# Expert and feed-forward work ordered with shorter matmul durations and no charge for a change of TensorE's array shape

## The chip, the cores and the metric

One core of one Trainium2 chip. The metric is the device time of one execution, in microseconds (us). The time before is 448.63 us, the median of 3 runs (446.47 to 449.24). TensorE appears in the trace as PE (matmuls) and PEld (weight loads), VectorE as DVE, ScalarE as ACT, GpSimd as POOL, and SyncE, which issues most of the transfers, as SP.

## The reference

Three layers, each feeding the next, on 1152 tokens of width 512:

```python
local = softmax(causal(q @ k.T / 8)) @ v                  # 2 x 8 heads, 576 tokens, width 64
out   = g * (phi(q) @ M_prev) / (phi(q) @ z_prev) + (1 - g) * local
e     = argmax(x @ w_gate)                                # one of 8 experts for each token, capacity 288
x     = gate_w * (relu(x @ w1[e]) @ w2[e])                # w1[e] 512 x 1024, w2[e] 1024 x 512
out   = ((x @ w_a) * (x @ w_b)) @ w_out                   # w_a, w_b 512 x 1536, w_out 1536 x 512 
```

The last layer's matrices are held as 64-bit numbers and arrive as pairs of 32-bit words.

## The kernel before

Attention and gating take the first 190 us or so and stay as they are. Then the experts run in an order that is set by how many tokens each has (a rank from 0 to 7; rank 0 is computed beside the attention), and then the feed-forward layer on the tokens that were kept. The program holds several versions of this part, for different token counts; the one that runs here is for up to 816 tokens with the last rank empty.

Of the experts that this part computes, rank 1 is "big" and split (each matmul operand is a high and a low part, and a product is three matmuls, lines 903 to 905, 288 columns wide); rank 2 is big in plain float32 (lines 1398 and 1434); ranks 3 to 6 are "few" (line 1491): the few tokens are the stationary operand in a slice of the array, 64 columns of it for rank 3 and 32 for ranks 4 to 6, and the result is turned by transposes (line 1500) after ACT has copied it out of PSUM (line 1496). Rank by rank, `few` has the steps fx (tokens turned, line 1479), f1 twice (first layer, one per half of w1), bt (transposes), fh (relu, line 1524), f2 twice (second layer), fy (copy out), bt, st and sl (high and low part into x2, lines 915 and 918).

The feed-forward layer goes over three blocks of 512 hidden columns (i = 0, 1, 2) and two stripes of tokens, 512 and 304 wide. For each block the halves of w_a, w_b and w_out (1 MB each) are loaded, rebuilt as float32 by ACT and DVE (s0 on ACT, line 1301; s1 to s3 on DVE, lines 1305 to 1315; then a high part on ACT, line 915, and a low part on DVE, line 918). For each stripe come four products pa with w_a and four pb with w_b, 12 matmuls each, then c1 (ACT copies pa out, line 1605), c2 (DVE multiplies with pb, line 1608), c3 and c4 (high and low part), and the products with w_out (om, or po in the last block; lines 1629 to 1631), added up by lines 1637 and 1639.

All of this is entered as a list of operations into a planner, `Plan`. Each operation has an engine, a duration, a key (a due time), the operations that it follows, and the buffers that it takes and uses. `Plan.run` picks operations one after the other by the engines' planned clocks and by key, and the instructions are emitted in that order. Each engine runs its instructions in order, so an instruction that waits holds up all that stand behind it on that engine. `Plan` also decides which of the load buffers (raw0, raw1, raws0, raws1, rawd0, rawd1 and three more) a transfer gets, and so which earlier operation must have ended before the transfer can be issued. Operations of `few` carry the mode 64 or 32, the others 0; where an operation's mode is not that of the one before on its engine, `run` adds `self.change` to the planned start.

Of the kernel before, what the change touches and what calls it, by code (L numbers as in the profile page):

```python
# [29 lines left out]
            w=280.2, w_=-166)  # L30
GK = 0.0
AHEAD_ = 0.094
CHANGE = 0.25
# [16 lines left out]
AH2 = 0.7  # L50
# [100 lines left out]
def fused_kernel(  # L151
# [350 lines left out]
    def stacked(i):  # L502
        return STACK and i == NF_
# [348 lines left out]
    def token_ids(key):  # L852
        nc.vector.tensor_tensor(out=big, in0=oh, in1=rs[:, 6][:, None, :].to_broadcast([128, NTT, E]), op=ALU.mult)
        nc.vector.reduce_sum(out=dst, in_=big, axis=AX.X)
        nc.vector.tensor_tensor(out=dst, in0=dst, in1=pos, op=ALU.add)
        nc.vector.tensor_tensor(out=dsi, in0=dst, in1=over, op=ALU.add)
        for t in range(NTT):
            M = rows[t % NT]
            scatter("id" + key, id_d, dsi[:M, t:t + 1], tid[:M, t:t + 1], N)
# [106 lines left out]
    for n, (b, p) in enumerate(pairs):  # L966
# [35 lines left out]
        for i in UNITS:  # L1002
            u = n, i
            at_ = n * UP + UNITS.index(i)
            W, one = 128 * i + rows[i], stacked(i)
# [41 lines left out]
    for b in range(B):  # L1047
        last = b == B - 1
        n = (b + 1) * NP - 1
        G = GROUPS if last else [(0, NT)]  # L1050
        for i in range(NT):
            t = b * NT + i
# [178 lines left out]
    class Way:  # L1231


        def __init__(self, pool, x2, more, buffers, held=()):

            self.x2, self.pool = x2, pool
            self.buffers = dict(buffers, raw=raw_cells, bank=banks,
                                u=[pool.tile([128, 2, 512], I32, name=f"u{n}") for n in range(2)])
            self.buffers["part"] = parts_ + self.buffers.get("part", [])
            self.held, self.tile = dict(held), {}  # L1240
            self.plan = Plan(dict({k: len(t) for k, t in self.buffers.items()}, any=more), AH2, ("raw", "part"), CHANGE)
            for b, slot in self.held.items():
                self.plan.hold(b, slot)
            self.op, self.stored = {}, []
# [111 lines left out]
        def big(self, r, c0, w, exact, key, f, kinds):  # L1356
# [1 line left out]

            job = r, c0
            cost = max(0.214, 1.667e-3 * w) if exact else 3.0e-3 * max(256, w) / 7.2 + 0.002  # L1360
            cost = cost if exact else 3 * (max(256, w) / 2400.0 + 0.0125)
            self.tokens(r, job, w, c0, key - 10, "raw")
            xs, xt, ht = ("xs", job), ("xt", job), ("ht", job)
            got = []
# [20 lines left out]
            t = key + f * 0.11 * 4 * -(-w // 128)  # L1385
# [173 lines left out]
        def forward(self, W, key, t, before):  # L1559
# [8 lines left out]
            tiles = cut(-(-W // 128))  # L1568
            for i in range(NI3):
                s_ = slice(512 * i, 512 * i + 512)  # L1570
                A, Bq, O = ((c, i) for c in "abo")
                A, Bq, O = (("ff", c, i) for c in "abo")
                per = sum(12 * (max(256, min(128 * n, W - 128 * sum(tiles[:g]))) / 2400.0 + 0.013) for g, n in enumerate(tiles))
                lasts = [0.0, 0.0]
                blocks_ = {}
                c0 = 0

                w0 = min(128 * tiles[0], W)
                one = 12 * (w0 / 2400.0 + 0.013)
                need = {A: t, Bq: t + (4 * one if i == 0 else one), O: t + 8 * one}  # L1580
                for blk, src in ((A, w_a[:, s_]), (Bq, w_b[:, s_]), (O, w_out[s_, :])):
                    blocks_[blk] = self.wide(blk, src, need[blk], None)
                for gi, n in enumerate(tiles):
                    w = min(128 * n, W - c0)
                    c = 12 * (max(256, w) / 2400.0 + 0.013)
                    early_ = i == 0 and gi == 0

                    def half(b, blk, m, w=w, c0=c0):
# [6 lines left out]
                    for m in range(4):  # L1595
                        a, b, av, g = (k_ + (i, gi, m) for k_ in (("pa",), ("pb",), ("av",), ("g",)))
# [68 lines left out]
    def cut(T):  # L1665
        n = -(-T // 4)
        return [T // n + (1 if j < T % n else 0) for j in range(n)]
# [58 lines left out]
    def general(exact):  # L1726
# [11 lines left out]
        with room("x2p") as xp:  # L1738
            x2 = xp.tile([128, KD, 2, N + max(256, -(-top // 32) * 32)], F32R, name="x2")
            for kk in range(KD):  # L1740
                nc.gpsimd.memset(x2[:, kk].bitcast(F32), 0.0)
            with room("mp") as mp, room("wp") as wp:
                h_ = mp.tile([128, 4, 2, SW], F32R, name="h_")
                buffers = {"xte": [mp.tile([128, KD, 128], F32, name="xte")],
                           "he": [[t[:, m] for m in range(8)] for t in [mp.tile([128, 8, 128], F32, name="he")]],
                           "xt": [xt0], "h": [[h_[:, m] for m in range(4)] + [h1[:, m] for m in range(4)]]}
                way = Way(wp, x2, 1, buffers)
                way.limited, t = False, 0.0
                for p in range(E):
                    small = exact and LIMITS[p] >= 5  # L1750
                    for c0 in [0] if small else range(0, top, SW):
                        way.big(RANKS[p], c0, 128 if small else min(SW, top - c0), small, t, 1.0,
                                ["xte" if small else "xt", "he" if small else "h"])
                        t += 30.0
                way.plan.run()
            choose(kept, [768, 960, N], forward)
# [41 lines left out]
```

## Time and profile before

| | us |
|---|---|
| median of 3 runs | 448.63 |
| the profiled execution | 454.4 |
| its span, first to last instruction | 452.6 |
| PE busy in the span | 407.4 |
| DVE busy in the span | 266.8 |
| ACT busy in the span | 208.4 |

The trace is of one execution, which took 454.4 us, 5.8 more than the median; 1.8 us of it lie outside the span. Start times in the rows count from the start of the span. A matmul's busy time overlaps the next one's, so what a stream of matmuls takes is read from the distance of their starts.

### The profile page before, as it was taken

The page shows a single profiled execution, that of the slowest core. Times are in us where ns is not written, and L with a number is a line of the kernel's source. Part 1 is how long each engine was busy: PE and PEld are TensorE (multiplying, and loading weights), DVE is VectorE, ACT ScalarE, POOL GpSimd, SP SyncE. Part 2 cuts the span into 40 slices and gives each one's busy share as a digit, 9 for nine tenths or more (in the row PEclk, how much of TensorE's full clock was granted, in tenths as well). Part 3 has the DMA queues.
Part 4 walks back from the last instruction along what each step waited for, and adds up shares of the span by engine and source line. Part 5 has one row for each costly group of instructions (what it writes and reads, how often), then busy time and mean ns, then how long its engine had stood idle before and what let it go on. Part 6 is the DMA issues. An engine that isn't in the chain of part 4 may idle for free.

```text
span 452.6 us, 7884 instructions
## 1 busy us (share of the span) xinstructions
PE 407.4 (90%) x2868; PEld 355.4 (79%) x2868; DVE 266.8 (59%) x639; ACT 208.4 (46%) x451; POOL 104.7 (23%) x182
## 2 busy tenths in 40 slices
PE   6789998988799999497799986999999999999993
PEld 6667887967687999485598964888978889788892
DVE  4567775598774685354035017686297883967231
ACT  3767887478875541352044033453355504434010
POOL 8683676056700004127000000000000000000202
PEclk9999998999989979699889996999999999999997
DMA  3688999837961005399999999924034000000101
GB/s 76 135 178 126 244 287 302 196 87 253 257 245 37 1 2 218 116 390 209 160 363 387 386 393 407 405 98 150 37 101 170 10 0 1 1 1 0 71 25 59
DMA packets 59912, 74.48 MB, mean 165 GB/s; under 512 B 33955, under 2 KB 33955, under 8 KB 59856
## 3 DMA queue, kind: packets, MB, share of 16 engines
q1 hardware_dynamic: 58016, 70.48, 51.0%
q0 software_dynamic: 1632, 3.31, 2.1%
q8 instruction: 27, 0.44, 0.4%
q14 instruction: 29, 0.24, 0.2%
q10 hardware_dynamic: 208, 0.01, 0.0%
HBM read 58.75 MB, written 11.64 MB: 156 GB/s over the span
## 4 chain that ended last, share of the span: by engine, by line
PE 42%; DMA 9%; issue 4%; POOL 1%; ACT 1%; POOLq 0%; SPq 0%
PE bank L903 9%; PE bank L904 9%; PE bank L905 9%; DMA rawd<-in_moe_w_dram 5%; PE bank L1629 3%; PE bank L1630 3%; PE bank L1631 3%; DMA raw<-in_moe_w_b_dram 3%; PE bank L1434 2%; PE bank L1491 2%; DMA raw<-xs_d 2%; POOL out_dram L762 1%; PE bank L1500 0%; PE bank L1479 0%; PE bank L912 0%
## 5 line engine op out<-in xcount | busy, mean ns | idle before, releaser
L905 PE MATMUL bank<-x,part 128*128 128x512 f32 (+1 forms) x192 | 67.6, 352 | 0.0
L903 PE MATMUL bank<-x,part 128*128 128x512 f32 (+1 forms) x160 | 56.7, 354 | 0.4 <-ACT x L915 0.4
L904 PE MATMUL bank<-x,part 128*128 128x512 f32 (+1 forms) x160 | 56.5, 353 | 0.0
L762 POOL DMA_INDIRECT out_dram<-c,ids x4 | 3.9, 986 | 200.3 <-DVE c L1639 196.8
L569 ACT ACTIVATE a<-sv,mn 128x128 f32<-128x128 f32 (+4 forms) x72 | 41.9, 584 | 16.5 <-DVE mn L549 15.5
L549 DVE CUSTOM_DVE_ANT_0 sv<-psS,mask 128x128 f32<-128x128 f32 (+4 forms) x72 | 34.5, 516 | 9.9 <-PE psS L533 7.6
L905 PEld LDWEIGHTS bank<-x,part 128*128 128x128 f32 x192 | 36.7, 191 | 4.3
L903 PEld LDWEIGHTS bank<-x,part 128*128 128x128 f32 x160 | 30.7, 192 | 4.5 <-issue 0.7
L904 PEld LDWEIGHTS bank<-x,part 128*128 128x128 f32 x160 | 30.8, 192 | 4.0 <-DVE x L918 0.2
L584 PE MATMUL psB<-ident,a 128*128 128x128 f32 x200 | 31.0, 282 | 2.3 <-ACT a L569 1.8
L1608 DVE TENSOR_TENSOR c<-c,bank 128x512 f32<-128x512 f32 (+1 forms) x24 | 13.9, 579 | 31.3 <-PE bank L905 30.9
L601 ACT COPY at<-psB 128x512 f32<-128x512 f32 (+2 forms) x48 | 23.7, 511 | 11.5 <-PE psB L584 9.0
L584 PEld LDWEIGHTS psB<-ident,a 128*128 128x128 f32 x200 | 23.8, 144 | 6.2 <-ACT a L569 3.4
L1605 ACT COPY c<-bank 128x512 f32<-128x512 f32 (+1 forms) x24 | 12.0, 500 | 27.5 <-PE bank L905 21.8
L915 ACT CAST a<-c 128x512 fp32r<-128x512 f32 (+1 forms) x12 | 6.4, 534 | 35.6 <-DVE c L1608 30.0
L611 PE MATMUL psC<-at,ldv 128*64 128x256 f32 (+1 forms) x192 | 19.9, 349 | 0.6 <-ACT at L601 0.6
L762 POOL DMA_INDIRECT xs_d<-x,di x10 | 10.5, 1046 | 40.8 <-DVE ggt L723 34.0
L533 PE MATMUL psS<-d 128*128 128x256 f32 (+2 forms) x56 | 16.1, 363 | 3.9 <-DMA d<-s 2.5
L918 DVE TENSOR_TENSOR part<-u,part 128x1024 fp32r<-128x1024 f32 x14 | 17.1, 1220 | 3.4 <-issue 1.9
L1305 DVE TENSOR_SCALAR u<-u 128x1024 f32<-128x1024 f32 x18 | 12.4, 687 | 11.2 <-ACT u L1301 11.2
L611 PEld LDWEIGHTS psC<-at,ldv 128*64 128x64 f32 x192 | 12.7, 136 | 7.2 <-issue 1.3
L918 DVE TENSOR_TENSOR x<-bank,x 128x160 f32 (+3 forms) x12 | 3.9, 363 | 22.7 <-ACT x L915 22.7
(293 smaller groups left out, 1105.3 us busy)
## 6 DMA issues: line engine op xcount, KB each, us to landing
raw<-in_moe_w_dram SPq DMA_DIRECT2D x16, 1024.0 KB, 9.9
rawd<-in_moe_w_dram SPq DMA_DIRECT2D x6, 1024.0 KB, 13.6
raws<-in_moe_w_dram SPq DMA_DIRECT2D x6, 1024.0 KB, 13.2
xs_d<-h SPq DMA_DIRECT2D x10, 512.0 KB, 3.9
d<-s SPq DMA_DIRECT2D x14, 288.0 KB, 3.5
rawd<-in_moe_w_a_dram SPq DMA_DIRECT2D x3, 1024.0 KB, 7.6
raw<-in_moe_w_b_dram SPq DMA_DIRECT2D x3, 1024.0 KB, 19.9
raws<-in_moe_w_out_dram SPq DMA_DIRECT2D x3, 1024.0 KB, 10.4
```

Source lines behind the costliest of these rows:

```text
L533: nc.tensor.matmul(sc[:M, h, 0:w], lhsT=l_, rhs=r_, start=j == 0, stop=j == 2)
L549: nc.vector.tensor_tensor_reduce(out=o, in0=i0, in1=i1, scale=1.0, scalar=3.0e38, op0=ALU.add, op1=ALU.min, accum_out=mn[:M])
L569: nc.scalar.activation(out=st[u, "a"][:M, h, 0:W], in_=sv[:M, 0:W], func=AF.Exp, scale=-1.0, bias=mn[:M], **more)
L584: nc.tensor.transpose(pt[:kr, M * j:M * j + M], a_t[:M, h, 128 * kt:128 * kt + kr], ident[:M, :M])
L601: eng(out=st[n, a, "at"][:, h0:h0 + nh, 0:i + 1, c0:c0 + 128], in_=pt[:, 0:m * 128].rearrange("p (h k m) -> p h k m", h=nh, m=128))
L611: nc.tensor.matmul(po[64 * h:64 * h + 64, c0:256], lhsT=vt[:, kt, h, 0:D], rhs=at_[:, h, kt, c0:256], start=kt == 0, stop=kt == 2 * a + 1)
L762: ins = nc.gpsimd.indirect_dma_start(out=out_[:, :], out_offset=bass.IndirectOffsetOnAxis(ap=idx, axis=0), in_=in_, in_offset=None, bounds ...
L903: nc.tensor.matmul(out_, lhsT=wh, rhs=xh, start=first, stop=False)
L904: nc.tensor.matmul(out_, lhsT=wh, rhs=xl, start=False, stop=False)
L905: nc.tensor.matmul(out_, lhsT=wl, rhs=xh, start=False, stop=last)
L918: (eng or nc.vector).tensor_tensor(out=to, in0=src, in1=hi, op=ALU.subtract)
L1608: nc.vector.tensor_tensor(out=self[av][:, 0:w], in0=self[av][:, 0:w], in1=self[b][:, 0:w], op=ALU.mult)
```

## The change

The planner for the experts and the feed-forward layer is made without the charge for a change of mode (0.25 us before, 0 now; the attention's planner keeps it), and three durations are shorter by 0.0098 or 0.010 us for each matmul. For a 512-wide feed-forward product that is 12 x (512/2400 + 0.003) in place of 12 x (512/2400 + 0.013) planned us; the due times (keys) of the feed-forward layer are sums of these and so shrink too. No instruction is added or removed in what runs; engines, shapes and data are the same.

```diff
-            self.plan = Plan(dict({k: len(t) for k, t in self.buffers.items()}, any=more), AH2, ("raw", "part"), CHANGE)
+            self.plan = Plan(dict({k: len(t) for k, t in self.buffers.items()}, any=more), AH2, ("raw", "part"))
...
-            cost = cost if exact else 3 * (max(256, w) / 2400.0 + 0.0125)
+            cost = cost if exact else 3 * (max(256, w) / 2400.0 + 0.0027)
...
-                one = 12 * (w0 / 2400.0 + 0.013)
+                one = 12 * (w0 / 2400.0 + 0.003)
...
-                    c = 12 * (max(256, w) / 2400.0 + 0.013)
+                    c = 12 * (max(256, w) / 2400.0 + 0.003)
```

Up to the start of the part for experts and feed-forward the instructions of every engine stand as before. In that part the first visible place is on ACT, where the experts end and the feed-forward layer begins. Before, in a row, from the last store of the rank-1 expert: line 1496 is fy, line 1524 fh, line 1301 s0 of w_b, lines 881 and 915 with x2 the store of the last expert, line 1605 c1:

```order
L915 COPY x2_4548<-bank4_2605 128x288
L1496 COPY c_4552<-bank2_2603 128x128
L1301 ACTIVATE u0_4554<-raws0_1917 128x1024
L1524 ACTIVATE c_4552<-bank3_2604 128x128
L1301 ACTIVATE u1_4555<-raw0_208 128x1024
L1496 COPY c_4552<-bank7_2608 128x128
L881 TENSOR_LOAD nums_204
L915 ISA
L915 COPY x2_4548<-bank5_2606 128x4x32
L915 CAST xt0_214<-u0_4554 128x1024
L1605 COPY c_4552<-bank0_2601 128x512
```

The same place of ACT after the change:

```order
L915 COPY x2_4549<-bank4_2605 128x288
L1496 COPY c_4553<-bank5_2606 128x128
L881 TENSOR_LOAD nums_204
L915 ISA
L915 COPY x2_4549<-bank1_2602 128x4x32
L1301 ACTIVATE u0_4555<-raw0_208 128x1024
L1605 COPY c_4553<-bank2_2603 128x512
L1301 ACTIVATE u1_4556<-raw2_5375 128x1024
L1605 COPY c_4553<-bank7_2608 128x512
L915 CAST part3_213<-u0_4555 128x1024
```

The two s0 of w_b now stand behind the last expert's copy and store; its relus (line 1524) have all moved up ahead of this piece, and the second s0 stands behind the first c1.

The second place is PE at the same point: the products of the experts of rank 5 and 6 (line 1491, 16 matmuls a row) and their transposes (line 1500), up to the first pa. Before:

```order
L1491 MATMUL bank2_2603<-raws1_2585,c_4552 32x128 x16
L1491 MATMUL bank2_2603<-rawd1_2593,c_4552 32x128 x16
L1491 MATMUL bank3_2604<-raw1_209,c_4552 32x128 x16
L1500 MATMUL bank5_2606<-ident_126,c_4552 128x128
L1500 MATMUL bank7_2608<-ident_126,c_4552 128x128
L1491 MATMUL bank2_2603<-rawd0_1977,c_4552 32x128 x16
L1500 MATMUL bank3_2604<-ident_126,c_4552 128x128
L1491 MATMUL bank7_2608<-raw1_5193,c_4552 32x128 x16
L1491 MATMUL bank7_2608<-raw0_5224,c_4552 32x128 x16
L1500 MATMUL bank5_2606<-ident_126,c_4552 128x128
L903 MATMUL bank0_2601<-x2_4548,part1_211 128x512
```

After, from one product further up:

```order
L1491 MATMUL bank2_2603<-raw1_209,c_4553 32x128 x16
L1500 MATMUL bank1_2602<-ident_126,c_4553 128x128
L1491 MATMUL bank7_2608<-raws1_2585,c_4553 32x128 x16
L1491 MATMUL bank5_2606<-rawd0_1977,c_4553 32x128 x16
L1491 MATMUL bank5_2606<-rawd1_2593,c_4553 32x128 x16
L1500 MATMUL bank1_2602<-ident_126,c_4553 128x128
L1500 MATMUL bank2_2603<-ident_126,c_4553 128x128
L1500 MATMUL bank7_2608<-ident_126,c_4553 128x128
L1491 MATMUL bank5_2606<-raw0_5238,c_4553 32x128 x16
L1491 MATMUL bank5_2606<-raw1_5281,c_4553 32x128 x16
L1500 MATMUL bank1_2602<-ident_126,c_4553 128x128
L903 MATMUL bank2_2603<-x2_4549,part1_211 128x512
```

Both f1 of rank 6 now come ahead of both f2 of rank 5; the last pair of products, the last transpose and the first pa follow each other as before.

The third place is ACT in the first block of the feed-forward layer; it shows in which order PE delivers (line 1605 copies pa out, line 1637 adds up the products with w_out). Before:

```order
L1605 COPY c_4552<-bank6_2607 128x512
L915 CAST h1_97<-c_4552 128x512
L915 CAST part3_213<-u1_4555 128x1024
L915 CAST h1_97<-c_4552 128x512
L1605 COPY c_4552<-bank0_2601 128x304
L1301 ACTIVATE u1_4555<-raw1_209 128x1024
L1637 COPY c_4552<-bank1_2602 128x512
```

After:

```order
L1605 COPY c_4553<-bank0_2601 128x512
L915 CAST h1_97<-c_4553 128x512
L1605 COPY c_4553<-bank3_2604 128x304
L915 CAST h1_97<-c_4553 128x512
L1605 COPY c_4553<-bank4_2605 128x304
L915 CAST part0_210<-u1_4556 128x1024
L1301 ACTIVATE u1_4556<-rawd0_1977 128x1024
L915 CAST a_4551<-c_4553 128x304
L915 CAST part2_5659<-u0_4555 128x1024
L1605 COPY c_4553<-bank1_2602 128x304
```

On PE two of the 304-wide pa of the second stripe stand right behind the four 512-wide pa, ahead of the first pb, and all but one product of the second stripe ahead of the first stripe's products with w_out; before, the first pb came after four pa, and the products with w_out after nine products in all. In blocks i = 1 and 2 PE's order is unchanged.

Earlier, among the experts: PE computes three of the rank-1 expert's last four products (b2, 24 matmuls each) ahead of the second layer of rank 4, where before it computed one there; and two weight blocks of rank 1 are loaded ahead of the first one of rank 4. The transfers of the two w1 halves of rank 6 still wait for the buffers that the second layer of rank 4 frees.

## Rows read from the trace of the kernel before

**Rows 1.** The page's transfers: engine, operation, count, KB of one, median us to landing.

```profile
d<-s SPq DMA_DIRECT2D x14, 288.0 KB, 3.5
```

**Rows 2.** Busy times by stretch: bounds, length, each engine (x instructions), clock, DMA, GB/s.

```profile
226.00:262.00 36.00, 35.12 (x370) 33.79 (x373) 10.29 (x16) 10.99 (x24) 0.77 (x1) 0.95 1.05 376
262.00:278.46 16.46, 9.88 (x246) 7.38 (x237) 5.45 (x9) 6.36 (x18) 0.00 (x0) 0.86 1.04 400
278.46:446.00 167.54, 167.28 (x828) 140.89 (x828) 110.09 (x140) 60.05 (x85) 5.89 (x6) 0.98 0.23 86
```

**Rows 3.** Timeline of PE: start, duration, what, [idle before <- releaser].

```profile
248.07 0.29 PE L905 MATMUL bank<-h,part 128*128 128x288 f32 x1
248.29 1.08 PE L1491 MATMUL bank<-raw,c 128*32 128x128 f32 x32
...
250.75 0.38 PE L903 MATMUL bank<-a,part 128*128 128x288 f32 x1
...
260.34 1.04 PE L1479 MATMUL bank<-ident,c 128*128 128x128 f32 x8
...
274.94 1.93 PE L1491 MATMUL bank<-raw,c 128*32 128x128 f32 x32 [3.45 <-ACT c L1524]
...
278.46 0.77 PE L903 MATMUL bank<-x,part 128*128 128x512 f32 x1 [0.45 <-ACT x L915]
...
283.81 0.53 PE L903 MATMUL bank<-x,part 128*128 128x512 f32 x1
```

**Rows 4.** Timeline of ACT, same columns.

```profile
273.60 1.12 ACT L1301 ACTIVATE u<-raws 128x1024 f32<-128x1024 f32 x1 [3.50 <-DMA raws<-in_moe_w_b_dram]
274.61 0.27 ACT L1524 ACTIVATE c<-bank 128x128 f32<-128x128 f32 x1
276.17 1.16 ACT L1301 ACTIVATE u<-raw 128x1024 f32<-128x1024 f32 x1 [1.28 <-DMA raw<-in_moe_w_b_dram]
277.22 0.27 ACT L1496 COPY c<-bank 128x128 f32<-128x128 f32 x1
278.05 0.27 ACT L915 CAST x<-bank 128x128 f32 x1 [0.57 <-PE bank L1500]
```

**Rows 5.** SP's timeline: an expert block, a w1 half of rank 6, the last expert block.

```profile
239.64 1.47 SPq L889 DMA_DIRECT2D raws<-in_moe_w_dram  x1
...
249.54 0.37 SPq L889 DMA_DIRECT2D raw<-in_moe_w_dram  x1
...
260.40 0.37 SPq L889 DMA_DIRECT2D raw<-in_moe_w_dram  x1
```

**Rows 6.** Transfers issued at 239.64 and at 260.40: KB, us from issue to landing.

```profile
raws<-in_moe_w_dram SPq DMA_DIRECT2D x1, 1024.0 KB, 13.2
...
raw<-in_moe_w_dram SPq DMA_DIRECT2D x1, 1024.0 KB, 10.6
```

**Rows 7.** TensorE's clock around the wait; columns as in Rows 2.

```profile
272.00:274.00 2.00, 0.00 (x0) 0.00 (x0) 0.00 (x0) 0.40 (x1) 0.00 (x0) 0.96 1.02 406
274.00:276.00 2.00, 1.06 (x20) 0.99 (x24) 1.22 (x2) 0.88 (x2) 0.00 (x0) 0.50 1.03 408
284.00:286.00 2.00, 2.00 (x10) 1.64 (x9) 0.31 (x1) 1.61 (x2) 0.00 (x0) 0.97 1.03 412
```

**Rows 8.** Timeline of PE at full clock: first 304-wide product, and what follows it.

```profile
303.17 0.30 PE L903 MATMUL bank<-x,part 128*128 128x304 f32 x1
...
304.85 0.39 PE L1629 MATMUL bank<-part,a 128*128 128x512 f32 x1
```

**Rows 9.** Timeline of DVE: w_b's first s1, last s3, last low part; w_out's last low part.

```profile
274.75 0.69 DVE L1305 TENSOR_SCALAR u<-u 128x1024 f32<-128x1024 f32 x1 [4.15 <-ACT u L1301]
...
282.52 1.23 DVE L1315 SCALAR_TENSOR_TENSOR u<-raw,u 128x1024 int32<-128x1024 int32 x1
...
288.46 1.22 DVE L918 TENSOR_TENSOR part<-u,xt 128x1024 fp32r<-128x1024 f32 x1 [1.34 <-ACT xt L915]
...
303.98 1.22 DVE L918 TENSOR_TENSOR part<-u,part 128x1024 fp32r<-128x1024 f32 x1
```

More of the change, by code (lines that the diff above doesn't have):

```diff
@@ L1572, in forward @@
                 A, Bq, O = (("ff", c, i) for c in "abo")
-                per = sum(12 * (max(256, min(128 * n, W - 128 * sum(tiles[:g]))) / 2400.0 + 0.013) for g, n in enumerate(tiles))
+                per = sum(12 * (max(256, min(128 * n, W - 128 * sum(tiles[:g]))) / 2400.0 + 0.003) for g, n in enumerate(tiles))
                 lasts = [0.0, 0.0]
```

## The prediction, made before the changed kernel ran

> **What bounds the kernel now.** I read the busy times by stretch first, then the timelines of PE and ACT at the one place where PE stands still, then the transfers that end there. Three stretches matter [rows 2]. From 226 to 262 us PE is busy 35.12 of 36 us and the transfer engines are full as well (DMA share 1.05). From 262 to 278.46 PE has work for only 9.88 of 16.46 us. From 278.46 to 446 it is busy 167.28 of 167.54 us: the feed-forward layer is a solid block of matmuls, and nothing but its start and its clock can shorten it. So the question is what sets 278.46.
>
> The timelines answer it. PE's last pair of expert products starts in full only at 274.94, after 3.45 us of waiting for the relu (line 1524) on ACT [rows 3]. That relu takes 0.27 us and runs at 274.61, because it stands behind the first s0 of w_b (line 1301), and that s0 waited 3.50 us for its transfer [rows 4]. The same again: the copy of the last product (line 1496) stands behind the second s0, which started at 276.17, after its own transfer. So the last expert waits for two feed-forward weights that it doesn't need. Its own last weight block had landed long before: issued at 260.40, 10.6 us to landing, 271.0 [rows 5, 6].
>
> The wait has a second cost. PE's clock fell from 1.00 (2.4 GHz) to 0.50 (1.2 GHz) behind the empty stretch and came back only from 284 us on [rows 7]. The first feed-forward product therefore took from 278.46 to 283.81, 5.35 us [rows 3].
>
> **The change part by part.** It removes and adds nothing; it moves.
>
> Edit 1, ACT: both s0 of w_b go behind the last store. Then the last pair can start when its weights are there, at 271.0. The pair of 16 takes 1.08 us at full clock (the x32 row at 248.29; 1.93 in the slow row) [rows 3], so 272.1. From the pair's end to the first feed-forward matmul it was 274.94 + 1.93 = 276.87 to 278.46, 1.6 us, which I keep. First pa at 273.7 if the landing stays, a gain of 4.8. Nothing new holds it: in the new order ACT has the four rank-1 stores ahead of the last copy, but these wait for PE products that end at 260.34 [rows 3], and PE's own f1 and f2 of rank 5 and 6 hold no more work than before.
>
> Edit 2, transfers: the w1 halves of rank 6 wait for the buffers of rank 4's second layer, and PE now has two more b2 products ahead of that. Three took from 250.75 to 260.34, 3.2 each [rows 3], so 6.4 us: the issue at 249.54 goes to 255.9. What is queued ahead of it: the block issued at 239.64 lands at 252.8 [rows 5, 6], then two more blocks and a quarter-block of tokens at 2.57 each (the distance of the two s0 of w_b, each released by its landing [rows 4]), so until 258.6. That leaves a lead of 2.7 us. A 288 KB transfer took 3.5 us to land [rows 1], some 2.8 beyond its own 0.7 of data at that rate, so the queue just about runs dry. I take 0.5 us of delay for every later landing, with ends at 0 and at one block's time, 2.6. Gain now 4.3; first pa at 274.2. The other loads that swap (two of rank 1 ahead of one of rank 4) lie in the stretch where PE is full and are used 5 us or more after landing; I cost them at 0, and about 1 us if one comes late.
>
> Edit 3, the clock: a 512-wide product is 2.75 us at full clock (5.35 at half, of which 2.6 is the price of the low clock). If PE no longer stands still for 3.45 us in one piece, the clock may hold. But the new order still leaves pauses of 1 to 2 us before the last two pairs, since they wait for landings. Between 0 and 2.6 us given back; I take 1.3. Forecast so far: 4.3 + 1.3 = 5.6 us.
>
> Edit 4, the first block: six pa instead of four before the first pb. Four at 2.75 and two 304-wide at 1.68 (303.17 to 304.85 [rows 8]) are 14.4 us, so the first pb comes at 288.6 us. It needs w_b's low parts. Before, the second was done at 289.7 [rows 9], and DVE was held up there by ACT's place behind c1. DVE's own work: s1 to s3 of both halves with the first low part ran from 274.75 to 283.75; the second low part is 1.22 more, and w_out's first s1, which now comes ahead of it, two instructions of 0.69 [rows 9]; that is 286.4, with hand-offs about 287. Cover of 1.6 us, and if it is gone, the excess is the cost. In the same way w_out's second low part ended at 305.2 [rows 9] while PE had begun its products with w_out at 304.85 [rows 8] without waiting, so these need the first half first; with all of the second stripe's products but one ahead of them they come at about 307, and DVE has w_out's second half by then or within 2 us. Cost 0. The rest of the block, and blocks 1 and 2, hold the same products, so a gain at 278.46 is a gain at the end.
>
> Shorter planned durations do not make a matmul shorter: 2.75 us for 12 is 0.229 each, 512/2400 = 0.213 plus 0.016, nearer to the old 0.013 than to the new 0.003. The Trainium skill (TensorE: Matmul & The Clock Gate, section "Wait — 56ns, not 53.3ns?") has N/2.4 GHz plus about 2.5 ns at full clock; the trace disagrees, with 16 ns here. By the page's figure the six pa would be an estimated 0.9 us shorter, and 0.9 us of edit 4's cover would be gone, with the same end.
>
> The shape changes, which the planner no longer charges: the last full-shape row at 248.07 to the first 32-column row at 248.29 is 0.22 where 0.13 is usual [rows 3], so 0.09 us a change. The count of runs of line 1491 between full-shape work is 8 before and 8 after, so 0. The Trainium skill (TensorEngine Tiling (Array Packing), section "Key Properties") says that changing the tiling mode drains the engine, which speaks against dropping the charge; the trace's 0.09 us agrees in kind, and with equal counts the rule costs nothing here.
>
> Sum against the profiled execution: 454.4 - 5.6 = 448.8. That execution is 5.8 above the median and I know no reason why this stretch should hold that excess, so the same 5.6 off the median: **443.0 us**.
>
> **The rivals.**
> (a) The transfers decide: rank 6's late loads let the queue run dry (2.6 instead of 0.5), or w_b's low parts come after the six pa (1 to 2). For it speaks the full DMA share; against it, the lead of 2.7 us. The gain shrinks to 1.5 to 3: 446.3.
> (b) The clock holds: all of 2.6 comes back and the queue doesn't run dry, 7.4 off: 441.2. For it, no pause as long as 3.45 us; against it, the pauses of 1 to 2 us that remain. It is part of the forecast's range.
> (c) No change: something else holds the last store until 278, for example ACT's rank-1 stores or a PSUM bank. Against it, ACT's row of 278.05, the last store, waited for the transpose alone, and no other work of ACT but the two s0 stands in between [rows 4]. 448.5.
> (d) Slower: the first block becomes DVE's. With c2 to c4 spread between w_b's, w_out's and the next w_a's steps and only two buffers av for pa's copies, PE waits for banks. A round c2, c3, c4, c1 serves two products, 5.5 us of PE; with two weight steps of 1.22 in it, it is about 6.3. If all 12 rounds of the layer were to overrun by 0.8, that is 9.6 lost and 4 us net, 452.6. It decides once a round has more than one weight step; against it, DVE is busy only 110 of 167.5 us there, and blocks 1 and 2 keep PE's order.
>
> **How the numbers follow.** The forecast has 0.66 (with (b) in it), (a) 0.19, (c) 0.08, (d) 0.07. The forecast's own range, 440.5 to 445, reaches from (b) with a little more to a gain of 3.6 (clock low as before, 0.7 more delay). With most of (a) the range is 440 to 447.5. About 1% is what a measurement of this kernel can tell from no change: 4.5 us, so faster means under 444.1. That is most of the forecast, 0.60, and nothing of the others; the rest of it, (a) and (c) give 0.33 within 1%; (d) 0.07.
>
> **What the profile would show.** Right: the first 512-wide matmul of line 903 at 273 to 275 us, line 1301 behind the last store on ACT, no wait of line 1491 for line 1524, PE full from there to the end at about 440. Edit 2: DMA share below 1.0 near 258 us, if it costs. Edit 3: how long the clock stays at 0.50 behind 272. Edit 4: an idle row of PE before the first pb, if it fails. Wrong: the first pa still near 278, or PE idle more than 2 us inside the feed-forward layer.

## The result, and the profile after

The changed kernel takes 444.07 us (median of 8 runs, 441.42 to 447.42), the kernel before 450.13 in the same comparison (8 runs): ratio 0.988, 95% interval 0.983 to 0.992. That is about 5.4 us, and faster by a little over 1%. The ratios here leave the slow runs out, so they need not be the quotient of the medians beside them. The profiled execution took 444.23 us with a span of 442.5.

The busy times by stretch of the changed kernel (columns as in [rows 2]):

```profile
226.00:262.00 36.00, 34.99 (x432) 32.93 (x430) 10.28 (x16) 11.58 (x27) 0.00 (x0) 1.00 1.05 381
262.00:274.00 12.00, 8.93 (x177) 7.17 (x178) 3.67 (x9) 4.55 (x14) 0.00 (x0) 1.00 1.04 401
274.00:300.00 26.00, 26.00 (x135) 22.53 (x134) 21.18 (x25) 13.20 (x17) 0.00 (x0) 1.00 0.71 282
300.00:436.00 136.00, 135.68 (x684) 114.04 (x682) 90.09 (x115) 47.98 (x69) 5.90 (x6) 1.00 0.17 59
```

The granted clock is 1.00 (2.4 GHz) in every one of them, where it was 0.50 in parts of the same place before [rows 7]. The timeline of PE of the changed kernel, from the last expert's first layer (263.34) and its last product (268.78) to the first pb:

```profile
263.34 1.08 PE L1491 MATMUL bank<-raws,c 128*32 128x128 f32 x32 [1.37 <-DMA raws<-in_moe_w_dram]
...
268.78 1.08 PE L1491 MATMUL bank<-raw,c 128*32 128x128 f32 x32 [0.81 <-DMA raw<-in_moe_w_dram]
270.24 0.33 PE L1500 MATMUL bank<-ident,c 128*128 128x128 f32 x1 [0.38 <-ACT c L1496]
271.01 0.48 PE L903 MATMUL bank<-x,part 128*128 128x512 f32 x1 [0.45 <-ACT x L915]
...
273.87 0.39 PE L903 MATMUL bank<-x,part 128*128 128x512 f32 x1
...
282.11 0.30 PE L903 MATMUL bank<-x,part 128*128 128x304 f32 x1
...
285.46 0.39 PE L903 MATMUL bank<-x,part 128*128 128x512 f32 x1
```

The last expert's last product now waits for a transfer, its own weights, and no longer for a relu on ACT [rows 3]. From the landing at 268.78 to the first feed-forward matmul it is 2.23 us. The first product takes 2.86 us (271.01 to 273.87), with its first matmuls a little slow; it took 5.35 before. ACT in the same place:

```profile
269.92 0.27 ACT L1496 COPY c<-bank 128x128 f32<-128x128 f32 x1 [0.99 <-PE bank L1491]
270.60 0.27 ACT L915 CAST x<-bank 128x128 f32 x1 [0.42 <-PE bank L1500]
271.24 1.13 ACT L1301 ACTIVATE u<-raw 128x1024 f32<-128x1024 f32 x1 [0.37 <-DMA raw<-in_moe_w_b_dram]
```

Copy and store of the last expert wait for PE alone; the first s0 of w_b comes behind them [rows 4].

The two spans differ by 10.1 us, more than the runs do. Part of this has nothing to do with the change. The turning of rank 2's tokens, in a stretch where every engine has the same order in both kernels, starts at 187.92 in the trace of before and 1.6 us earlier in the trace of after (the first row is before's):

```profile
187.92 1.94 PE L912 MATMUL bank<-ident,raws 128*128 128x128 f32 x8 [5.99 <-DMA raws<-xs_d]
186.31 1.94 PE L912 MATMUL bank<-ident,raws 128*128 128x128 f32 x8 [6.63 <-DMA raws<-xs_d]
```

So I read two distances that don't depend on where this starts. **Landing to first pa**: from the landing of the last expert's last weights to the first matmul of the feed-forward layer. Where the trace doesn't show that landing, it is taken as 2.45 us ahead of the first s0 of w_b, if that s0 was released by its own landing (2.45 is the distance in the experiment with the early s0, below, which shows both: 269.83 and 272.28; above it is 268.78 and 271.24, which is the same). **First pa to end**: from there to the end of the span. Before: 273.60 - 2.45 = 271.15 to 278.46, 7.31 us; and 452.6 - 278.46 = 174.1. After: 2.23 and 442.5 - 271.01 = 171.5. By these the change gives 5.1 + 2.6 = 7.7 us.

### The profile page after: what moved, and what is told of

Its sections match the earlier page's. It is cut to its first block, busy times and chain, and to the rows that moved or that the text cites. A ratio compares the mean times of both kernels' runs of the same rounds, so it can differ in the third digit from the quotient of the medians.

```text
span 442.5 us, 7877 instructions
## 1 busy us (share of the span) xinstructions
PE 401.5 (91%) x2868; PEld 350.6 (79%) x2868; DVE 265.4 (60%) x639; ACT 208.5 (47%) x451; POOL 103.9 (23%) x182
## 4 chain that ended last, share of the span: by engine, by line
PE 63%; DMA 13%; DVE 6%; issue 6%; ACT 5%; POOL 4%; SPq 1%; POOLq 0%; ACTq 0%; DVEq 0%
PE bank L903 9%; PE bank L905 9%; PE bank L904 9%; DMA rawd<-in_moe_w_dram 5%; DMA raw<-in_moe_w_dram 5%; PE bank L1629 4%; PE bank L1630 4%; PE bank L1631 3%; ACT a L569 3%; PE psC L684 2%; PE bank L1398 2%; PE psC L611 2%; PE psB L584 2%; PE psS L533 2%; PE bank L1434 2%
## 5 line engine op out<-in xcount | busy, mean ns | idle before, releaser
L903 PE MATMUL bank<-x,part 128*128 128x512 f32 (+1 forms) x192 | 66.7, 347 | 0.4 <-ACT x L915 0.4
L904 PE MATMUL bank<-x,part 128*128 128x512 f32 (+1 forms) x192 | 66.5, 346 | 0.0
L905 PE MATMUL bank<-x,part 128*128 128x512 f32 (+1 forms) x160 | 55.5, 347 | 0.0
L762 POOL DMA_INDIRECT out_dram<-c,ids x4 | 4.0, 988 | 192.6 <-DVE c L1639 189.1
L903 PEld LDWEIGHTS bank<-x,part 128*128 128x128 f32 x192 | 36.1, 188 | 4.9 <-issue 0.6
L904 PEld LDWEIGHTS bank<-x,part 128*128 128x128 f32 x192 | 36.1, 188 | 4.3
L905 PEld LDWEIGHTS bank<-x,part 128*128 128x128 f32 x160 | 30.1, 188 | 3.4
L915 ACT CAST part<-u 128x1024 fp32r<-128x1024 f32 x16 | 16.7, 1049 | 12.0 <-DVE u L1315 12.0
L918 DVE TENSOR_TENSOR part<-raw,part 128x1024 fp32r<-128x1024 f32 x12 | 14.8, 1254 | 6.1 <-ACT part L915 6.1
```

Source lines behind the costliest of these rows:

```text
L903: nc.tensor.matmul(out_, lhsT=wh, rhs=xh, start=first, stop=False)
L904: nc.tensor.matmul(out_, lhsT=wh, rhs=xl, start=False, stop=False)
L905: nc.tensor.matmul(out_, lhsT=wl, rhs=xh, start=False, stop=last)
L915: nc.scalar.copy(out=to, in_=src)
L918: (eng or nc.vector).tensor_tensor(out=to, in0=src, in1=hi, op=ALU.subtract)
```

## The experiments

For the first three, the planner is left as it is, and its finished order is edited: named operations are taken out of their engine's queue and put in elsewhere, all else keeps its order.

**Only ACT's place of the two s0, in the kernel before.** Both s0 of w_b go behind the last expert's last store. The order then wants one move on DVE as well (the last expert's low part ahead of w_b's first s1). Transfers and PE's order stay as before.

```diff
...
+                o, b0, end = way.op, ("ff", "b", 0), (6, 0)
+                way.plan.moves = [(o["s0", b0, n], o["st", end], True) for n in (1, 0)]
+                way.plan.moves += [(o["sl", end], o["s1", b0, 0], False)]
```

> The kernel before with one edit: on ACT both s0 of w_b stand behind the last expert's store, and on DVE the last expert's low part ahead of w_b's first step; PE, SP and all else as before. Theory (ACT's place holds the last expert): this alone gives the whole gain of the change, first feed-forward matmul 2 to 3 us after the last expert block has landed (7.5 before), 5 to 8 us faster than before, about 444. Rival (the other moves count, PE's six first products or the order of the loads): at most half of it, 447 or slower.

Measured: 445.77 us (441.54 to 449.2, 6 runs) against 449.87, ratio 0.988, interval 0.982 to 0.994. ACT's timeline, and then PE's first pa:

```profile
270.03 0.27 ACT L1534 COPY c<-bank 128x128 f32<-128x128 f32 x1 [1.95 <-PE bank L1529]
270.71 0.27 ACT L953 CAST x<-bank 128x128 f32 x1 [0.42 <-PE bank L1538]
271.35 1.13 ACT L1339 ACTIVATE u<-raws 128x1024 f32<-128x1024 f32 x1 [0.38 <-DMA raws<-in_moe_w_b_dram]
```

```profile
271.12 0.47 PE L941 MATMUL bank<-x,part 128*128 128x512 f32 x1 [0.45 <-ACT x L953]
```

(In the three edited orders line numbers are 38 higher from here on.) The first pa starts 0.23 us ahead of the first s0, exactly as in the changed kernel (271.01 and 271.24), and the rest takes 442.8 - 271.12 = 171.7. This one edit gives as much as the whole change. The move on DVE came with it; that the gain is not DVE's is what the next experiment shows, where ACT's two s0 alone go back.

**The two s0 put back ahead of the last copy, in the changed kernel.** All else of the change stays.

```diff
...
+                o, b0, end = way.op, ("ff", "b", 0), (6, 0)
+                way.plan.moves = [(o["s0", b0, n], o["fy", end, 2], False) for n in (0, 1)]
```

> The changed kernel with one edit undone: on ACT both s0 of w_b stand ahead of the last expert's copy again; PE, SP and DVE as after the change. Theory: the copy waits for the second half of w_b, first feed-forward matmul 7 to 8 us after the last expert block's landing, the clock falls again, and the whole gain is lost: 448 to 451, no different from before. Rival (the other moves count): it keeps half of the gain or more, 447 or faster.

Measured: 449.94 us (446.1 to 455.92, 12 runs), ratio 0.998 (0.994 to 1.001). PE waits as it did before, though the order of its own work is that of the changed kernel; PE, then ACT:

```profile
269.83 1.08 PE L1529 MATMUL bank<-raw,c 128*32 128x128 f32 x32 [0.83 <-DMA raw<-in_moe_w_dram]
276.15 0.47 PE L1538 MATMUL bank<-ident,c 128*128 128x128 f32 x1 [5.24 <-ACT c L1534]
277.07 0.77 PE L941 MATMUL bank<-x,part 128*128 128x512 f32 x1 [0.45 <-ACT x L953]
```

```profile
272.28 1.11 ACT L1339 ACTIVATE u<-raw 128x1024 f32<-128x1024 f32 x1 [2.31 <-DMA raw<-in_moe_w_b_dram]
274.82 1.12 ACT L1339 ACTIVATE u<-raw 128x1024 f32<-128x1024 f32 x1 [1.43 <-DMA raw<-in_moe_w_b_dram]
275.85 0.25 ACT L1534 COPY c<-bank 128x128 f32<-128x128 f32 x1
```

The last product was done at about 270.9; the copy of its result runs at 275.85, behind two s0 that wait for landings. Landing to first pa is 277.07 - 269.83 = 7.24 again, and the clock is 0.50 from 274 to 282; the last of these stretches:

```profile
280.00:282.00 2.00, 2.00 (x6) 1.52 (x6) 1.97 (x3) 0.00 (x0) 0.00 (x0) 0.50 1.03 412
```

By the trace the gain is gone; by the interval of the ratio at most 0.6% can be left, half of what the change gave.

**The clock alone, in the kernel before.** PE's waits in the last expert are filled with 13, 6 and 2 matmuls of 512 columns into the bank that the first pa will overwrite. They are extra work for PE; nothing is left out.

```diff
...
+                def keep_on(n):
+                    wh = way.pair(("ff", "a", 0))[0]
+                    for _ in range(n):
+                        nc.tensor.matmul(way["pa", 0, 0, 0], lhsT=wh[:, 0, 0:128], rhs=wh[:, 0, :], start=True, stop=True)
...
+                way.plan.extra = {o["f2", end, 0]: lambda: keep_on(13), o["f2", end]: lambda: keep_on(6),
+                                  o["bt", end, 2]: lambda: keep_on(2)}
```

> The kernel before with matmuls whose results nobody reads in PE's wait: 13 of 512 columns after the first of the last two expert products, 6 after the second, 2 after the last transpose. The wait stays, 278 us in the profile of before. Theory (the fallen clock costs 2.6 us on its own): granted clock 1.00 through the wait, first feed-forward product 2.75 in place of 5.35 us, 2 to 3 us faster, about 447.5. Rival (the clock is not worth it, or the added matmuls are in the way): within 1 us of before.

Measured: 448.65 us (445.39 to 450.58, 12 runs), ratio 0.9955 (0.992 to 0.999). The busy times by stretch (the extra matmuls are in PE's share), and the first s0 on ACT and the first pa:

```profile
262.00:274.00 12.00, 10.84 (x185) 8.14 (x176) 5.41 (x9) 5.41 (x14) 0.00 (x0) 1.00 1.03 406
274.00:286.00 12.00, 12.00 (x52) 9.63 (x52) 10.82 (x14) 6.08 (x8) 0.00 (x0) 1.00 1.03 408
```

```profile
269.17 1.13 ACT L1339 ACTIVATE u<-raws 128x1024 f32<-128x1024 f32 x1 [2.75 <-DMA raws<-in_moe_w_b_dram]
```

```profile
274.15 0.47 PE L941 MATMUL bank<-x,part 128*128 128x512 f32 x1
```

The clock stays at 1.00, and the first pa to the end takes 445.7 - 274.15 = 171.6 in place of 174.1. The hold on ACT is still there: 4.98 us from the first s0 to the first pa, 4.86 before [rows 3, 4]. So the clock's share is 2.5 us by the traces and 2.0 by the medians (0.4 to 3.6), and it can be had without the other.

**The changed kernel again**, on the same chip as the three above.

> The changed kernel once more beside the others. Theory: 6 us faster than before again, about 444; the profile with the clock at 1.00 from 262 us on and the last block's landing 2 to 3 us ahead of the first feed-forward matmul. Rival (the first profile was a lucky one in the clock): the wait is gone but the clock falls, 4 to 5 us faster.

Measured: 445.86 us (443.33 to 450.75, 6 runs), ratio 0.989 (0.983 to 0.995). It is level with the kernel that has ACT's edit alone.

**One half of the change: only the charge dropped** (the durations as before).

```diff
-            self.plan = Plan(dict({k: len(t) for k, t in self.buffers.items()}, any=more), AH2, ("raw", "part"), CHANGE)
+            self.plan = Plan(dict({k: len(t) for k, t in self.buffers.items()}, any=more), AH2, ("raw", "part"))
```

In the order that this gives, one s0 of w_b stands ahead of the last expert's copy and the other behind its store.

> Only the charge for a change of shape is dropped; the durations stay. In this order the first s0 of w_b stands ahead of the last expert's copy, the second behind its store, and PE has four pa ahead of the first pb as before. Theory (each s0 ahead of the last expert's store costs the wait for its transfer): the first feed-forward matmul comes 2.6 us (one block) later than in the changed kernel, some 5 us after the last expert block's landing; 2.4 us faster than before, up to 5 if the clock holds. Rival (dropping the charge is the whole effect): as fast as the changed kernel, 444.

Measured: 446.72 us (445.35 to 451.4, 12 runs) against 449.01 there, ratio 0.9945 (0.991 to 0.998). One s0 on ACT, and PE's wait behind it:

```profile
269.08 1.12 ACT L1301 ACTIVATE u<-raw 128x1024 f32<-128x1024 f32 x1 [2.33 <-DMA raw<-in_moe_w_b_dram]
270.10 0.26 ACT L1496 COPY c<-bank 128x128 f32<-128x128 f32 x1
270.92 0.27 ACT L915 CAST x<-bank 128x128 f32 x1 [0.57 <-PE bank L1500]
```

```profile
270.41 0.48 PE L1500 MATMUL bank<-ident,c 128*128 128x128 f32 x1 [2.69 <-ACT c L1496]
271.33 0.77 PE L903 MATMUL bank<-x,part 128*128 128x512 f32 x1 [0.45 <-ACT x L915]
```

One s0 in the way costs half of two: 271.33 - (269.08 - 2.45) = 4.70 us from landing to first pa, 2.5 above the changed kernel's 2.23. The clock is still lost (0.50 from 272 to 276; the first half of it):

```profile
272.00:274.00 2.00, 1.88 (x5) 1.49 (x5) 1.97 (x3) 0.79 (x1) 0.00 (x0) 0.50 1.02 406
```

**The other half: only the three durations.**

```diff
-            cost = cost if exact else 3 * (max(256, w) / 2400.0 + 0.0125)
+            cost = cost if exact else 3 * (max(256, w) / 2400.0 + 0.0027)
...
-                one = 12 * (w0 / 2400.0 + 0.013)
+                one = 12 * (w0 / 2400.0 + 0.003)
...
```

The lines of the third duration and of the due times have the same edit. Both s0 stay in the way, one ahead of the copy and one ahead of the store.

> Only the three durations are shortened; the charge stays. In this order the first s0 of w_b stands ahead of the last expert's copy, and the second ahead of its store. Theory: the store waits for both transfers, as before; first feed-forward matmul 7 us after the last expert block's landing, within 1 us of before. Rival (the durations are the effect): as fast as the changed kernel.

Measured: 449.37 us (445.4 to 454.57, 12 runs), ratio 0.999 (0.995 to 1.003): no difference that the runs can tell. ACT, then PE:

```profile
272.43 1.12 ACT L1301 ACTIVATE u<-raw 128x1024 f32<-128x1024 f32 x1 [1.66 <-DMA raw<-in_moe_w_b_dram]
273.44 0.26 ACT L1496 COPY c<-bank 128x128 f32<-128x128 f32 x1
274.99 1.14 ACT L1301 ACTIVATE u<-raws 128x1024 f32<-128x1024 f32 x1 [1.29 <-DMA raws<-in_moe_w_b_dram]
276.03 0.25 ACT L915 CAST x<-bank 128x128 f32 x1
```

```profile
276.43 0.76 PE L903 MATMUL bank<-x,part 128*128 128x512 f32 x1 [2.35 <-ACT x L915]
```

**More traces of the two kernels.** The medians give some 5.4 us, the first pair of traces 7.7. Is the hold there in every execution? Both kernels were profiled again, unedited.

> The kernel before, unchanged, for a second trace of it. Two distances are read: from the start of the first s0 of w_b (line 1301, released by its transfer) to the first feed-forward matmul (4.86 us in the first trace), and from there to the span's end (174.1 us). If ACT's order holds the last expert in every execution, the first distance is 4.5 to 5.2 again, whatever the transfers' times, and the second 174 with the low clock. If the hold varies from execution to execution, which would explain why the medians gave 5.4 us where the two traces give 7.7, the first lies below 4 or the second near 171.6 in one of the two new traces.

> The kernel before once more, with the same two readings as for the second trace: 4.5 to 5.2 and 174 if the hold and the low clock are there each time; below 4 or near 171.6 if not.

> The changed kernel, unchanged, for a third trace. If ACT's order is all, the first matmul of the feed-forward layer starts 0.2 us ahead of the first s0 of w_b and the rest takes 171.5 to 171.8 us, as in the first two traces. If the clock is only just held over the pauses that remain, the rest is near 174 in some execution; then the median's gain is smaller than the traces'.

The second trace of before (448.18 us): the first s0, the first pa, and the place ahead of the changed part, which started 6 us earlier than in the first trace (187.92).

```profile
267.85 1.11 ACT L1301 ACTIVATE u<-raws 128x1024 f32<-128x1024 f32 x1 [1.49 <-DMA raws<-in_moe_w_b_dram]
```

```profile
181.96 1.94 PE L912 MATMUL bank<-ident,raws 128*128 128x128 f32 x8 [5.54 <-DMA raws<-xs_d]
...
272.68 0.77 PE L903 MATMUL bank<-x,part 128*128 128x512 f32 x1 [0.45 <-ACT x L915]
```

The hold is 272.68 - 267.85 = 4.83 us, though rank 2's work started 6 us earlier. All traces by the two distances, with what the sum is against the mean of before's three (181.3):

| kernel | landing to first pa | first pa to end | sum against before, us | measured ratio |
|---|---|---|---|---|
| before, three traces | 7.31, 7.28, 7.31 | 174.1, 173.7, 174.2 | 0 | 1 |
| after, three traces | 2.23, 2.23, 2.24 | 171.5, 171.7, 171.3 | -7.6 | 0.988, 0.989 |
| s0 late, in before | as after | 171.7 | -7.4 | 0.988 |
| s0 early, in after | 7.24 | 174.1 | 0 | 0.998 |
| clock alone, in before | 7.43 | 171.6 | -2.3 | 0.9955 |
| charge alone | 4.70 | 174.6 | -2.0 | 0.9945 |
| durations alone | 6.45 | 173.8 | -1.1 | 0.999 |

In the unedited kernels the two distances repeat within 0.1 and 0.5 us; what scatters lies ahead of them.

## Why the prediction held

**Edit 1, ACT's order (4.8 us taken): right, 5.1.** Moving the two s0 alone gives the whole gain (0.988), putting them back takes it all (0.998), and one of two in the way costs half. What was taken for the stretch from the landing to the first pa, 1.08 + 1.6, is 2.23. The prediction calls the x32 row a pair of 16; it is one product, whose 16 matmuls stand as 32 records in the trace, and as only one waits for the landing, the sum stands. The first pa at 271.01 is ahead of the 273 to 275 named as a sign: the landing came at 268.78 and not at 271.0, and the stretch is shorter by 0.45.

**Edit 2, transfers (0.5 taken, ends 0 and 2.6): nothing that can be told from 0.** PE's order did delay the two w1 halves, from 249.54 and 250.49 to 252.19 and 253.15, but the transfer engines had no pause, in windows of the changed kernel around the place named:

```profile
254.00:258.00 4.00, 3.01 (x24) 2.78 (x24) 0.29 (x1) 0.53 (x2) 0.00 (x0) 1.00 1.05 386
258.00:262.00 4.00, 3.97 (x102) 3.10 (x102) 0.00 (x0) 0.99 (x4) 0.00 (x0) 1.00 1.05 386
```

The issue came 3.7 us earlier than the 255.9 worked out, 1.6 of them because this execution was that much earlier at rank 2's start already; the delay that PE's order made was thus about 4.3 us in place of 6.4. From the row of line 912 to the last landing it is 82.5, 83.9 and 81.7 us in the three traces after and 83.2, 83.4 and 80.1 before: 0.5 more on average, with a scatter of 3. And the kernel that has before's transfers with ACT's new order is level with the changed one. The 0.5 us in the sum were for a pause that did not come.

**Edit 3, the clock (1.3 taken between 0 and 2.6): mis-sized, it gave back 2.5 to 2.6, all of it.** The pauses that remain (1.37 and 0.81 us in the first trace, 1.35 and 0.85 in the third, 0.97 in the second) did not lower it. The prediction could not tell whether they would and took half of the term. Two effects with one cause: taking the hold away takes the clock's loss away too, and the clock alone is worth 2.0 to 2.5.

**Edit 4, the first block (0): right.** Six pa take 271.01 to 285.46, 14.45 us (14.4 forecast). The second low part of w_b on DVE is done by 284.48, so the cover is 1.0 us against 1.6 forecast, and PE shows no wait between 271.5 us and its last matmul at 435.28:

```profile
283.26 1.22 DVE L918 TENSOR_TENSOR xt<-u,part 128x1024 fp32r<-128x1024 f32 x1
```

**Durations and charge.** Neither changed a matmul. From 273.87 on a 512-wide matmul of the changed kernel is 0.229 us (36 of them to 282.11), as before. By the page TensorE: Matmul & The Clock Gate of the Trainium skill, section "Wait — 56ns, not 53.3ns?", a matmul of this width would be an estimated 13 ns shorter; the measurement stands against it. Both halves were only inputs to a sort, and their effects don't add up: 2.0 and 1.1 us by the traces, 7.6 together, because only the two together put both s0 behind the store.

**The sum.** 5.6 us was forecast, 443.0 from a median of 448.63. The runs gave 5.4 (3.4 to 7.5), the traces 7.6. Rival (b) describes the traces, with the clock held and the queue full; (a), (c) and (d) fell: no delay of transfers that can be told from 0, the last store at 270.6 in place of 278.05, and PE without a wait from 271.5 to its last matmul at 435.28. That 5.6 met the 5.4 of the runs is in part luck: with the terms as the traces measured them (5.1, 0, 2.5 to 2.6 and 0) the same sum gives 7.6 to 7.7. Why the medians give about 2 us less than the two distances stays open; 7.6 is at the edge of the interval. The whole spans of the three traces of each kernel average 448.9 and 443.1 us, 5.7 apart: the last landing came 1.9 us later on average in the changed kernel's traces, and 1.4 of that were there already at the start of rank 2's work, where both kernels still have the same order. That start scatters from 182.0 to 189.1 us over all traces, so this can be chance; no run here holds it still.

## What to carry to other kernels

Where an engine waits for a short instruction of another, look at what stands ahead of that instruction in the other's queue: two preparations of later work, each held by its own transfer, cost five microseconds here although ACT was busy less than half of the time. Order a work step that waits for a transfer behind whatever the bottleneck engine still needs, as long as the step's own reader has the time (here 1.0 us of it was left). Judge an edit of a planner's numbers by the order that it gives at the one place where the bottleneck stands idle; that two planned costs are nearer to or farther from the measured ones says nothing by itself.

## What the runs showed of the hardware

The clock was either kept, or lost for most or all of the first feed-forward product. With one s0 in the way PE's wait was 2.69 us and the first product ran at 0.50; with pauses of 1.37 and 0.81 us the clock stayed at 1.00. But a wait of 2.69 us or more isn't needed for the loss: in the second trace of before no wait of PE there was longer than 1.49 us, with a product of 1.08 us between the two longest, and the clock fell all the same. PE, then the busy times by stretch, in that trace:

```profile
269.19 1.08 PE L1491 MATMUL bank<-raw,c 128*32 128x128 f32 x32 [1.43 <-ACT c L1524]
271.76 0.47 PE L1500 MATMUL bank<-ident,c 128*128 128x128 f32 x1 [1.49 <-ACT c L1496]
```

```profile
274.00:278.00 4.00, 4.00 (x11) 3.08 (x11) 3.97 (x4) 0.03 (x1) 0.00 (x0) 0.53 1.02 407
```

What does decide it stays open here. The price of the low level, as the first pa to the end against the changed kernel's 171.5, was 2.2 to 3.1 us at the start of a layer that runs for about 165 us almost without a pause.

A good part of the scatter arises ahead of the changed part: three executions of the same program reached the same instruction at 187.92, 181.96 and 185.99 us, and their times were 454.4, 448.18 and 449.35. The order of the three is the same, the distances are not: 4.0 us between the second and the third start became 1.2 in the times.
